# A new slot plan for windowed attention followed by a two-layer SMELU network

## The chip, the core and the metric

The kernel runs on one core of a Trainium2 chip. The metric is device time in microseconds, from the launch of the program to its end, as the median of several runs. One execution was also taken by the hardware profiler; its page and trace are read here.

The engines by their names in the profile: PE is TensorE (matmuls; PEld its weight loads), ACT is ScalarE, DVE is VectorE, POOL is GpSimd, SP is SyncE. In this kernel POOL issues all loads and SP issues the stores and the transposing transfers.

## What is computed

```python
# q, k, v: 8 batches, 8 heads, 576 positions, 64 wide
scores = matmul(q, k.T) / sqrt(64)
scores = where(|i - j| <= 32, scores, -1e9)
attn = exp(scores - max) / sum(exp(scores - max))
x = matmul(attn, v)              # regrouped to 4608 tokens x 512
h = x @ w_in                     # 512 x 2048
g = where(h >= 1, h, where(h <= -1, 0, (h + 1)**2 / 4))
out = g @ w_out                  # 2048 x 512, result 4608 x 512
```

## The kernel before

**Slots.** The kernel is one long list of 160 numbered slots, written out by hand (L505 to L566), because the order in which instructions are written is the order in which each engine runs them. Slots 0 to 143 each make one 128x512 tile of h: a projection on TensorE (L499: eight matmuls of 256 columns; in the wide slots 56 to 135 L524: four of 512) and then its SMELU. The last 16 slots have no projection left.

**SMELU, two forms.** Always ScalarE first: rr = relu(h/2 + 1/2) (L543). Then either VectorE does both of max(h, rr) and min(rr, 1) times that (L549, L550), or, in the slots named in `two_on_act`, ScalarE squares rr (L546) and VectorE does one instruction (L547). I call these Square slots. The tile of h lies in PSUM in one of two buffers, so the projection of slot a+2 waits until slot a's readers, rr and the max (or L547), are done.

**Products with w_out.** `unit` (L459) is one matmul of 512 columns of the second layer, `pair` (L474) eight matmuls of 256 columns, used early while only half of w_out is loaded. They come after the projection of a slot. Sixteen units make one 128x512 tile of the result; ScalarE copies it out of PSUM and SP stores it. Before: four units per slot in slots 24 to 39 (through `post`), three in 40 to 71, four after. The slot of each pair is listed in `pairs`.

**Attention events.** `scores` (L231, exponent on ScalarE L239, band mask, and the helper sum `both` on VectorE, L244) and `sums` (L304: numerators and denominators; then Ln and Exp of the denominator on ScalarE, L310 and L311, and a product on VectorE, L316, that writes xT) are put at positions by `at`; position a is after the projection of slot a, a + 0.5 after its products. `seq` lists, for batches 1 to 7, five sums and five scores each; `sl` gives the slots of the later ones. The product into xT is held back in `muls` and issued by `flush` at the next slot's start. `run` issues the events of a position: the matmuls of all of them, the scores with their Exp, and then, in a loop at the end, Ln and Exp of each sums.

**The mask, two forms.** With `eng` None the mask is added on TensorE by four extra matmuls (`add_mask`, L210); else VectorE multiplies the exponentials by a 0/1 mask (L205), which GpSimd prepares once (L156 to L159). Before: TensorE in slots under 14.

**Transfers.** Loads are issued by POOL in written order (L133 to L161). Eight completion semaphores take turns, so an issue waits until the one eight earlier has landed. For batch 0 q and k come in halves (`load_half`), for batch 1 in rows (`load_rows`), both transposed on TensorE (`tposes`, L191); from batch 2 on `load_nat` loads them as they lie and `xpose` (L198) transposes them by a DMA that SP issues, at the slots in `xps`. SP runs its stores and transposes in written order. q buffers of one batch and k buffers of the next take turns, so a load waits for the transpose that read the buffer before.

Of the kernel before, what the change touches and what calls it, by code (L numbers as in the profile page):

```python
# [14 lines left out]
def kernel(  # L15
# [20 lines left out]
    B, H, S, D = q.shape  # L36
    NT, DM, DFF = out.shape[0], 512, 2048
# [3 lines left out]
    MAIN = 480  # L41
    TAIL = S - MAIN
# [7 lines left out]
    nat = ctx.enter_context(tc.tile_pool(name="nat", bufs=2))  # L50
# [6 lines left out]
    ps_s = ctx.enter_context(tc.tile_pool(name="ps_s", bufs=1, space=bass.MemoryType.PSUM))  # L57
    ps_n = ctx.enter_context(tc.tile_pool(name="ps_n", bufs=1, space=bass.MemoryType.PSUM))
# [44 lines left out]
    def load_v(b, n):  # L103
        if b not in vn:
            vn[b] = nat.tile([128, 2 * NC, 2, D], BF, name="vn", tag="vn", bufs=3)
        h, a = divmod(n, 2)
        y = NY * h + 2 * a
        nc.gpsimd.dma_start(out=vn[b][64 * a:64 * a + 64, :, h], in_=v[b, y:y + 2].rearrange("y s d -> (y s) d")  # L108
                            .rearrange("(c r) d -> r c d", r=64))
# [15 lines left out]
    for h in range(2):  # L125
# [8 lines left out]
    load_v(0, 0)  # L134
    P.affine_select(out=step, in_=step, compare_op=ALU.is_ge, fill=-1.0, base=-65, channel_multiplier=-1,
                    pattern=[[1, 257]])
    for n in range(1, 4):
        load_v(0, n)
    V.memset(ones, 1.0)
    for t in qTs:  # L140
        V.memset(t[:, 0:PAD], 0.0)
# [1 line left out]
    V.tensor_sub(band, step[:, 65:], step[:, :192])  # L143
    V.tensor_scalar(bias, band, 1.0, 2.0 ** 100, op0=ALU.subtract, op1=ALU.mult)

    def put(todo):
        for fn, *x in todo:
            fn(*x)

    cuts = [0, 256, 512, 768, 1024, 1280, 1536, DFF]  # L150
    w = [(load_w_in, c0, c1, h) for c0, c1 in zip(cuts, cuts[1:]) for h in range(2)]
    w[3] += ((0, 52, 64),)
    put(w[:4] + [(load_half, 1, t, h) for t in range(2) for h in range(2)] + w[4:])
    put([(load_w_out, 0, k, k + 4) for k in (0, 4, 8)] + [(load_rows, 1, t) for t in range(2)] + [(load_w_out, 0, 12, 16)])
    put([(load_v, 1, n) for n in range(4)])
    P.tensor_copy(band[HD[1], 0:128], band[HD[1], 64:192])  # L156
    for m, n, x in ((mask4, 8, 128), (mask8, 4, TAIL)):
        P.tensor_copy(m.rearrange("p (n j) -> p n j", n=n),
                      band[:, :x].rearrange("p (n j) -> p n j", n=1).to_broadcast([128, n, x]))  # L159
    put([(load_w_out, 1, 8 * n, 8 * n + 8) for n in range(2)])  # L160
    put([(load_nat, 2, t) for t in range(2)] + [(load_v, 2, n) for n in range(4)])  # L161


    kT = {}

# [161 lines left out]
    TB = 256  # L327
# [55 lines left out]
    ps_o = ctx.enter_context(tc.tile_pool(name="ps_o", bufs=2, space=bass.MemoryType.PSUM))  # L383
# [3 lines left out]

    NB = NT // TB
    NF = DFF // 256
    pairs = [(7, 0), (7, 1), (8, 2), (11, 4), (12, 5), (13, 3), (15, 6), (15, 8), (16, 7), (17, 9)]  # L390
    two_on_act = (1, 7, 10, 11, 12)
    ev = {}

    def at(a, *todo):


        ev.setdefault(a, []).extend(x for x in todo if x)

    def steps(b, cut):

        for k, (lo, hi) in enumerate(((0, cut), (cut, MAIN))):
            for y1 in range(2):
                yield (sums, b, y1, lo, hi), (scores, b, (y1, y1 + 1), (0, 2), (2 * k, 2 * k + 2))
        yield (sums, b, 0, MAIN, S), (scores8, b)

    at(1, (tposes, 0, (0, 1), (1, 1)))
    at(2, (scores, 0, (0, 1), (0, 2), (2, 4)), (scores8, 0, ps_o))
    at(3, (scores, 0, (1, 2), (0, 2), (2, 4), ps_n), (sums, 0, 0, TB, MAIN, ps_s))
    at(4, (sums, 0, 1, TB, MAIN))
    at(5, (sums, 0, 0, MAIN, S, ps_s))  # L410
    seq = [x for b in range(1, B) for x in steps(b, CUT)]
    at(12.5, seq[0][1])
    at(13, (*seq[1][1], ps_n))
    at(14, (*seq[0][0], ps_s), seq[1][0])
    at(16, seq[2][1])
    for n, a in enumerate((18, 20, 26.5, 28)):
        at(a, seq[2 + n][0])
    for n, a in enumerate((18, 20, 26.5, 28)):
        at(a, seq[3 + n][1])
    sl = [30, 32, 35, 39, 42, 45, 47, 50, 52, 57, 60, 63, 66, 68, 72, 76, 79, 82, 86]  # L420
    sl += [90, 93, 96, 100, 104, 108, 111, 114, 118, 123]
    for n, a in enumerate(sl):
        at(a, seq[6 + n][0], seq[7 + n][1] if n < len(sl) - 1 else None)
    for t in range(2):
        at(10 + 1.5 * t, (tposes, 1, (t, 0), (t, 1)))
    two_on_act += tuple(a + 2 for a in sl)
    loads, xps = {}, {16: [(2, 0)], 18: [(2, 1)]}
    for b in range(LONG + 1, B):
        a = sl[5 * (b - 1) - 7] - 17
        for t in range(3):  # L430
            loads.setdefault(a + t, []).append((b, t))
        for t in range(2):
            xps.setdefault(a + 6 + 2 * t, []).append((b, t))

    op = {}

# [46 lines left out]
    def run(pos):  # L483
        todo = []
        for fn, *x in ev.get(pos, []):
            if fn is sums:
                todo.append(sums(*x))
            elif fn is tposes:
                tposes(*x)
            else:  # L490
                pool = (x.pop(),) if x[-1] in (ps_s, ps_n, ps_o) else ()
                fn(*x, eng, *pool)
        for end in todo:
            end()

# [5 lines left out]
                             skip_group_check=True)  # L501

    hps = []
    done = 4 * (40 - NF)
    for a in range(NF * NB + 2 * NF):  # L505
        wide = WIDE[0] <= a < WIDE[1]
        eng = None if a < 14 else V
        post = [] if a >= 40 else [x for n, x in pairs if n == a] + [a - NF] * (a >= 2 * NF + 2)
        for b, x in loads.get(a, []):
            if x < 2:  # L510
                load_nat(b, x)
            else:
                for n in range(4):
                    load_v(b, n)
        if a == 0 or a > 3:
            flush()
        if a < NF * NB:
            if wide:
                n, f = divmod(a - WIDE[0], 2 * NF)
                t = WIDE[0] // NF + 2 * n  # L520
                r0 = TB * t % RING
                hp = ps_h.tile([128, 2, TB], FP, name="hp", tag="hp")
                for n, kk in enumerate((0, 2, 1, 3)):
                    nc.tensor.matmul(hp.rearrange("p n t -> p (n t)"), w_in[:, kk, 128 * f:128 * f + 128],  # L524
                                     xT[:, kk, r0:r0 + 2 * TB], start=n == 0, stop=n == 3)
                g = gT[:, f, home(t):home(t + 1) + 1:home(t + 1) - home(t)]
            else:
                t, f = divmod(a, NF)
# [12 lines left out]

            rr = ewp.tile([128, 2, TB], FP, name="rr")
            A.activation(rr, hp, AF.Relu, scale=0.5, bias=0.5)  # L543
            mx = ewp.tile([128, 2, TB], FP, name="mx")
            if a in two_on_act:
                A.activation(mx, rr, AF.Square)  # L546
                V.scalar_tensor_tensor(g, hp, 1.0, mx, op0=ALU.max, op1=ALU.min)  # L547
            else:
                V.tensor_max(mx, hp, rr)  # L549
                V.scalar_tensor_tensor(g, rr, 1.0, mx, op0=ALU.min, op1=ALU.mult)  # L550
        flush()
        run(a)
        for x in post:
            if x < 16:
                pair(x)
            else:
                for j in range(4):
                    unit(4 * x + j)
        if a >= 40:
            n = 3 if a < 72 else 4  # L560
            for x in range(done, done + n):
                unit(x)
            done += n
        run(a + 0.5)
        for x in xps.get(a, []):
            xpose(*x)  # L566
# [30 lines left out]
```

## Time and profile before

| | |
|---|---|
| median of 3 runs | 307.9 us (307.62 to 308.05) |
| profiled execution | 307.01 us, span 305.2 us from first to last instruction |
| granted TensorE clock | 1.000 |
| SMELU max L549, product L550 | 110 each, 689 and 694 ns |
| SMELU Square L546, product L547 | 34 each, 630 and 690 ns |
| ScalarE rr L543 | 144, 594 ns |
| mask product L205 | 33; 686 ns for 128x1024, 352 ns for 128x384 |
| scores' Exp L239 | 33; 1022 ns for 128x1024 |
| bias matmuls L210 | 32 |

The page gives for each engine the busy time, then the chain of work that ended last, followed back from the last instruction, then groups of instructions by line with what ended the idle time ahead of them. A line such as `26.12 1.92 PE hp L499 x16` of the chain is start, duration, engine, tile, line and count, all in microseconds from the span's start. The end of a matmul in the trace is modelled, its start is measured. A transfer's landing is the last of its completion updates.

The start of a slot is the start of its projection's first matmul: slot 2 at 18.38, slot 6 at 26.12, slot 14 at 42.33, slot 26 at 66.08, slot 32 at 78.82, slot 40 at 95.63, slot 72 at 152.52, slot 124 at 253.19 us.

### The profile page before, as it was taken

How to read it: one execution, taken by the hardware profiler on the slowest of the kernel's cores; microseconds unless marked ns; L12 is line 12 of the kernel's file. 1: busy time of each engine (PE TensorE's matmuls, PEld its weight loads, DVE VectorE, ACT ScalarE, POOL GpSimd, SP SyncE). 2: the span in 40 equal slices, each digit the busy share in tenths (PEclk: the TensorE clock that was granted, in tenths of full speed). 3: DMA queues.
4: the chain of work that ended last, by engine and by line, in shares of the span. 5: the costliest groups of instructions: out<-in, count | busy, mean ns of one | idle time of the engine just before them, and what ended most of it. 6: DMA issues, size and time to landing. Idle time of an engine off the chain costs nothing.

```text
span 305.2 us, 7779 instructions
## 1 busy us (share of the span) xinstructions
PE 296.6 (97%) x3268; PEld 172.1 (56%) x3268; DVE 232.4 (76%) x377; ACT 208.0 (68%) x347; POOL 77.5 (25%) x93
## 2 busy tenths in 40 slices
PE   8889999999999999999999999999999999999995
PEld 3467878876566667545444444444445444446644
DVE  4269878989888898999888878877888877788700
ACT  3677786738877888788877877786778755444311
POOL 8895771019008107303700640000000000000000
PEclk9999999999999999999999999999999999999999
DMA  9999999999999999996999998570101000000121
GB/s 151 182 180 200 187 183 172 173 165 147 135 213 90 172 159 128 150 147 121 165 133 156 120 173 82 113 114 34 37 34 38 37 35 37 35 34 34 63 77 69
DMA packets 137251, 35.66 MB, mean 117 GB/s; under 512 B 122240, under 2 KB 132992, under 8 KB 137216
## 3 DMA queue, kind: packets, MB, share of 16 engines
q0 software_dynamic: 103056, 18.06, 80.5%
q1 hardware_dynamic: 34016, 16.81, 27.2%
q8 instruction: 25, 0.41, 0.6%
q10 hardware_dynamic: 144, 0.29, 0.4%
q14 instruction: 10, 0.08, 0.1%
HBM read 36.70 MB, written 9.44 MB: 151 GB/s over the span
## 4 chain that ended last, share of the span: by engine, by line
PE 84%; DMA 4%; DVE 4%; POOL 4%; ACT 2%; issue 1%; POOLq 0%; ACTq 0%
PE op L459 33%; PE hp L524 23%; PE hp L499 14%; PE op L474 5%; PE bb L304 5%; DMA w_in<-in_moe_w_in_dram 4%; POOL w_in L113 2%; PE bb L231 2%; DVE mx L549 1%; PE op L450 1%; POOL vn L108 1%; ACT pt L239 1%; DVE gT L550 1%; PE tp L191 1%; DVE xT L316 1%
## 5 line engine op out<-in xcount | busy, mean ns | idle before, releaser
L543 ACT ACTIVATE rr<-hp 128x512 f32<-128x512 f32 x144 | 85.5, 594 | 68.5 <-PE hp L524 37.7
L459 PE MATMUL op<-w_out,gT 128*128 128x512 bf16 x496 | 127.0, 380 | 0.0
L549 DVE TENSOR_TENSOR mx<-hp,rr 128x512 f32<-128x512 f32 x110 | 75.8, 689 | 26.1 <-ACT rr L543 25.3
L524 PE MATMUL hp<-xT,w_in 128*128 128x512 bf16 x320 | 82.1, 379 | 0.0
L550 DVE SCALAR_TENSOR_TENSOR gT<-rr,mx 128x512 bf16<-128x512 f32 x110 | 76.4, 694 | 3.8
L459 PEld LDWEIGHTS <-gT 128*128 128x128 bf16 x496 | 46.0, 98 | 47.6
L499 PE MATMUL hp<-xT,w_in 128*128 128x256 bf16 x512 | 66.4, 273 | 3.3 <-DMA w_in<-in_moe_w_in_dram 2.1
L499 PEld LDWEIGHTS <-w_in 128*128 128x128 bf16 x512 | 49.1, 98 | 19.0 <-issue 3.2
L524 PEld LDWEIGHTS <-w_in 128*128 128x128 bf16 x320 | 31.2, 98 | 38.2 <-issue 0.9
L100 POOL DMA_DIRECT2D qn<-in_q_dram x12 | 14.6, 1223 | 91.7 <-DMA kT<-kn 89.6
L239 ACT ACTIVATE pt<-bb 128x1024 bf16<-128x1024 f32 (+1 forms) x33 | 32.8, 999 | 3.5 <-PE bb L231 2.2
L547 DVE SCALAR_TENSOR_TENSOR gT<-hp,mx 128x512 bf16<-128x512 f32 x34 | 23.5, 690 | 13.9 <-ACT mx L546 13.6
L108 POOL DMA_DIRECT2D vn<-in_v_dram x32 | 27.5, 893 | 6.1 <-DMA w_out<-in_moe_w_out_dram 3.2
L463 ACT COPY osb<-op 128x512 f32<-128x512 f32 x31 | 18.0, 579 | 12.0 <-PE op L459 11.6
L316 DVE TENSOR_TENSOR xT<-bb,rc 128x512 bf16<-128x512 f32 (+1 forms) x32 | 20.9, 654 | 5.7 <-ACT rc L311 5.6
L311 ACT ACTIVATE rc<-lr 128x512 f32<-128x512 f32 (+2 forms) x40 | 23.5, 588 | 1.3
L310 ACT ACTIVATE lr<-bb 128x512 f32<-128x512 f32 (+2 forms) x40 | 22.0, 550 | 0.2 <-PE bb L304 0.2
L546 ACT ACTIVATE mx<-rr 128x512 f32<-128x512 f32 x34 | 21.4, 630 | 1.1
L205 DVE TENSOR_TENSOR pt<-pt,mask 128x1024 bf16<-128x1024 bf16 (+1 forms) x33 | 20.3, 615 | 1.4 <-ACT pt L239 1.4
L304 PE MATMUL bb<-pt,vn 64*64 64x128 bf16 (+3 forms) x712 | 18.7, 207 | 0.0
L304 PEld LDWEIGHTS <-vn 64*64 64x64 bf16 x712 | 14.7, 107 | 4.9 <-issue 4.7
L474 PE MATMUL op<-w_out,gT 128*128 128x256 bf16 x128 | 16.4, 273 | 0.0
(63 smaller groups left out, 167.2 us busy)
## 6 DMA issues: line engine op xcount, KB each, us to landing
out_dram<-osb SPq DMA_DIRECT2D x35, 256.0 KB, 2.8
vn<-in_v_dram POOLq DMA_DIRECT2D x32, 144.0 KB, 11.2
qn<-in_q_dram POOLq DMA_DIRECT2D x12, 288.0 KB, 6.2
kn<-in_k_dram POOLq DMA_DIRECT2D x12, 288.0 KB, 8.8
w_in<-in_moe_w_in_dram POOLq DMA_DIRECT2D x11, 128.0 KB, 5.1
w_out<-in_moe_w_out_dram POOLq DMA_DIRECT2D x4, 256.0 KB, 9.2
w_out<-in_moe_w_out_dram POOLq DMA_DIRECT2D x2, 512.0 KB, 12.3
kh<-in_k_dram POOLq DMA_DIRECT2D x4, 144.0 KB, 5.1
```

The costliest lines, as they stand in the source:

```text
L108: nc.gpsimd.dma_start(out=vn[b][64 * a:64 * a + 64, :, h], in_=v[b, y:y + 2].rearrange("y s d -> (y s) d") .rearrange("(c r) d -> r c d", ...
L239: A.activation(p, ps[:, :, :w * n].rearrange(like, y=m), AF.Exp, scale=D ** -0.5)
L304: nc.tensor.matmul(bb[HD[h], a, o + c0:o + c1], ones[HD[a]] if c is None else vn[b][HD[a], c, h], p(a, h), start=n == 0, stop=True, skip_g ...
L311: A.activation(rc[:, :, :D0], lr[:, :, :D0], AF.Exp, scale=-1.0)
L316: muls.append(lambda: V.tensor_mul(o, bb[:, :, :D0], rc[:, :, :D0]))
L459: nc.tensor.matmul(op[tt], gT[:, j, home(tt // 2), 128 * (tt % 2):128 * (tt % 2) + 128], w_out[:, j], start=j == 0, stop=j == 15)
L474: nc.tensor.matmul(o[:, tt], gT[:, j, p, 128 * tt:128 * tt + 128], w_out[:, j, 256 * half:256 * half + 256], start=not done, stop=len(done ...
L499: nc.tensor.matmul(hp[:, j], w_in[:, kk, 256 * f + 128 * j:256 * f + 128 * j + 128], xT[:, kk, r0:r0 + TB], start=first and n == 0, stop=l ...
L524: nc.tensor.matmul(hp.rearrange("p n t -> p (n t)"), w_in[:, kk, 128 * f:128 * f + 128], xT[:, kk, r0:r0 + 2 * TB], start=n == 0, stop=n == 3)
L543: A.activation(rr, hp, AF.Relu, scale=0.5, bias=0.5)
L549: V.tensor_max(mx, hp, rr)
L550: V.scalar_tensor_tensor(g, rr, 1.0, mx, op0=ALU.min, op1=ALU.mult)
```

## The change

The plan is written anew, as tables; the work itself (projections, SMELU tiles, products, scores, sums, transfers) is the same set.

- `LOADS` names every load in order. One half of the first w_in block goes ahead of the last three value tiles of batch 0; the halves of batch 0 and the w_in blocks from 768 on are interleaved differently; one value tile of batch 1 goes ahead of the last w_out block of the first half; k of batch 2 comes before q, with a value tile between.
- Masks on VectorE from position 11.5 on, instead of slot 14.
- Events: transposes of batch 0's second half at 0.5 instead of 1; the sums of slots 4 and 5 together at 5.5; the scores of 12.5 and 13 together at 12.5; those of 16 at 15.5; 18 and 20 become 18.5 and 20.5; at 28 the scores come before the sums; a new list `sl` of the same 29 entries.
- `two_on_act` is a list of its own, 27 slots instead of 34.
- `pairs` names all sixteen pairs (before, the last six followed from the slot number), and `units` gives the number of w_out products of each slot, 0 to 7, in all 512 as before.
- `ends_first`: at these positions Ln and Exp of a sums are issued right after its matmuls, ahead of the scores that follow in the same event.
- The transposes of later batches (`xps`) get slots of their own, k before q for batch 2; the loads of a batch (`loads`) too.

```diff
+    LOADS = [('w', 0, 256, 0), ('v', 0, 1), ('v', 0, 3), ('v', 0, 2), ('w', 0, 256, 1), ('w', 256, 512, 0), ('w', 256, 512, 1, (0, 52, 64)), ('half', 1, 0, 1), ('half', 1, 1, 0), ('half', 1, 0, 0), ('half', 1, 1, 1), ('w', 512, 768, 0), ('w', 512, 768, 1), ('w', 1024, 1280, 0), ('w', 768, 1024, 1), ('w', 768, 1024, 0), ('w', 1280, 1536, 0), ('w', 1280, 1536, 1), ('w', 1024, 1280, 1), ('w', 1536, 2048, 0), ('w', 1536, 2048, 1), ('o', 0, 0, 4), ('o', 0, 4, 8), ('o', 0, 8, 12), ('rows', 1, 0), ('rows', 1, 1), ('v', 1, 0), ('o', 0, 12, 16), ('v', 1, 3), ('v', 1, 2), ('v', 1, 1), ('masks',), ('o', 1, 0, 8), ('o', 1, 8, 16), ('nat', 2, 1), ('v', 2, 1), ('nat', 2, 0), ('v', 2, 2), ('v', 2, 3), ('v', 2, 0)]
...
-    for n in range(1, 4):
-        load_v(0, n)
...
-    put(w[:4] + [(load_half, 1, t, h) for t in range(2) for h in range(2)] + w[4:])
-    put([(load_w_out, 0, k, k + 4) for k in (0, 4, 8)] + [(load_rows, 1, t) for t in range(2)] + [(load_w_out, 0, 12, 16)])
-    put([(load_v, 1, n) for n in range(4)])
...
-    put([(load_nat, 2, t) for t in range(2)] + [(load_v, 2, n) for n in range(4)])
...
+    for kind, *x in LOADS:
+        kinds[kind](*x)
...
-    pairs = [(7, 0), (7, 1), (8, 2), (11, 4), (12, 5), (13, 3), (15, 6), (15, 8), (16, 7), (17, 9)]
-    two_on_act = (1, 7, 10, 11, 12)
+    pairs = [(6, 0), (7, 1), (8, 2), (11, 4), (12, 5), (13, 3), (14, 6), (15, 8), (17, 7), (17, 10), (18, 9), (19, 13), (19, 15), (21, 14), (22, 11), (23, 12)]
...
-    sl = [30, 32, 35, 39, 42, 45, 47, 50, 52, 57, 60, 63, 66, 68, 72, 76, 79, 82, 86]
-    sl += [90, 93, 96, 100, 104, 108, 111, 114, 118, 123]
...
-    two_on_act += tuple(a + 2 for a in sl)
-    loads, xps = {}, {16: [(2, 0)], 18: [(2, 1)]}
+    for a, *names in [(0.5, 't0'), (2, 'c0', 'c2'), (3, 'c1', 's0'), (5.5, 's1', 's2'), (10, 'tq'), (11.5, 'tk'), (12.5, (1, 0), 'C1'), (14, 'S0', (0, 1)), (15.5, (1, 2)), (18.5, (0, 2), (1, 3)), (20.5, (0, 3), (1, 4)), (26.5, (0, 4), (1, 5)), (28, (1, 6), (0, 5))]:
...
+    two_on_act = [6, 10, 11, 13, 16, 22, 25, 28, 30, 34, 41, 44, 47, 51, 59, 62, 64, 74, 90, 96, 109, 122, 123, 126, 127, 131, 132]
+    sl = [30, 35, 37, 39, 42, 45, 47, 49, 52, 58, 60, 63, 65, 68, 71, 77, 79, 81, 85, 89, 92, 95, 101, 103, 108, 110, 112, 115, 117]
+    first_sl = 6
+    bias_until = 11.5
+    ends_first = [0.5, 2.5, 3, 4, 10, 11.5, 12.5, 14, 15.5, 20, 36, 49, 75, 89, 93, 116, 118, 123]
...
+    for t, a in enumerate([16, 15]):
+        xps.setdefault(a, []).append((2, t))
...
-            xps.setdefault(a + 6 + 2 * t, []).append((b, t))
+            xps.setdefault([[28, 30], [40, 44], [58, 59], [75, 79], [91, 98]][b - 3][t], []).append((b, t))
...
             if fn is sums:
                 todo.append(sums(*x))
+                if pos in ends_first:
+                    todo.pop()()
...
-                fn(*x, eng, *pool)
+                fn(*x, None if pos < bias_until else V, *pool)
...
+    units = [0, 0, 0, 0, 0, 0, 0, 0, 0, 0, 0, 0, 0, 0, 0, 0, 0, 0, 0, 0, 0, 0, 0, 0, 5, 3, 5, 4, 5, 3, 6, 5, 0, 4, 4, 5, 4, 4, 3, 3, 3, 4, 3, 3, 3, 3, 2, 4, 3, 1, 5, 3, 2, 3, 4, 3, 2, 3, 4, 2, 4, 3, 3, 3, 4, 3, 3, 2, 4, 3, 4, 1, 4, 6, 2, 5, 2, 4, 5, 3, 4, 4, 5, 4, 6, 2, 2, 7, 2, 4, 6, 4, 4, 2, 4, 3, 5, 4, 5, 4, 6, 1, 3, 6, 4, 5, 4, 3, 3, 5, 5, 2, 4, 7, 2, 4, 0, 4, 5, 6, 3, 6, 3, 7, 4, 2, 5, 4, 3, 4, 4, 4, 4, 4, 5, 4, 2, 4, 6, 3, 4, 3, 4, 4, 5, 2, 4, 4, 6, 5, 4, 5, 3, 2, 3, 3, 4, 7, 4, 4]
...
-        eng = None if a < 14 else V
-        post = [] if a >= 40 else [x for n, x in pairs if n == a] + [a - NF] * (a >= 2 * NF + 2)
...
-        if a >= 40:
-            n = 3 if a < 72 else 4
-            for x in range(done, done + n):
-                unit(x)
-            done += n
+        for x in range(done, done + units[a]):
+            unit(x)
+        done += units[a]
```

More of the change, by code (lines that the diff above doesn't have):

```diff
@@ L144, with masks @@
     V.tensor_scalar(bias, band, 1.0, 2.0 ** 100, op0=ALU.subtract, op1=ALU.mult)
[L146 to L152, printed above, removed]
-    put(w[:4] + [(load_half, 1, t, h) for t in range(2) for h in range(2)] + w[4:])
-    put([(load_w_out, 0, k, k + 4) for k in (0, 4, 8)] + [(load_rows, 1, t) for t in range(2)] + [(load_w_out, 0, 12, 16)])
-    put([(load_v, 1, n) for n in range(4)])
[L156 to L160, printed above, removed]
-    put([(load_nat, 2, t) for t in range(2)] + [(load_v, 2, n) for n in range(4)])
+    def masks():
+        P.tensor_copy(band[HD[1], 0:128], band[HD[1], 64:192])
+        for m, n, x in ((mask4, 8, 128), (mask8, 4, TAIL)):
+            P.tensor_copy(m.rearrange("p (n j) -> p n j", n=n),
+                          band[:, :x].rearrange("p (n j) -> p n j", n=1).to_broadcast([128, n, x]))
+    kinds = {"v": load_v, "w": load_w_in, "half": load_half, "o": load_w_out, "rows": load_rows, "nat": load_nat, "masks": masks}
+    for kind, *x in LOADS:
+        kinds[kind](*x)
     kT = {}
@@ L404, in steps @@
         yield (sums, b, 0, MAIN, S), (scores8, b)
[L406 to L410, printed above, removed]
-    seq = [x for b in range(1, B) for x in steps(b, CUT)]
[L412 to L419, printed above, removed]
-    sl = [30, 32, 35, 39, 42, 45, 47, 50, 52, 57, 60, 63, 66, 68, 72, 76, 79, 82, 86]
-    sl += [90, 93, 96, 100, 104, 108, 111, 114, 118, 123]
-    for n, a in enumerate(sl):
-        at(a, seq[6 + n][0], seq[7 + n][1] if n < len(sl) - 1 else None)
-    for t in range(2):
-        at(10 + 1.5 * t, (tposes, 1, (t, 0), (t, 1)))
-    two_on_act += tuple(a + 2 for a in sl)
@@ L427 @@
-    loads, xps = {}, {16: [(2, 0)], 18: [(2, 1)]}
+    seq = [x for b in range(1, B) for x in steps(b, CUT)]
+    early_items = {"t0": (tposes, 0, (0, 1), (1, 1)), "c0": (scores, 0, (0, 1), (0, 2), (2, 4)), "c2": (scores8, 0, ps_o),
+                   "c1": (scores, 0, (1, 2), (0, 2), (2, 4), ps_n), "s0": (sums, 0, 0, TB, MAIN, ps_s),
+                   "s1": (sums, 0, 1, TB, MAIN), "s2": (sums, 0, 0, MAIN, S, ps_s),
+                   "tq": (tposes, 1, (0, 0), (0, 1)), "tk": (tposes, 1, (1, 0), (1, 1)),
+                   "C1": (*seq[1][1], ps_n), "S0": (*seq[0][0], ps_s)}
@@ new lines @@
+    for a, *names in [(0.5, 't0'), (2, 'c0', 'c2'), (3, 'c1', 's0'), (5.5, 's1', 's2'), (10, 'tq'), (11.5, 'tk'), (12.5, (1, 0), 'C1'), (14, 'S0', (0, 1)), (15.5, (1, 2)), (18.5, (0, 2), (1, 3)), (20.5, (0, 3), (1, 4)), (26.5, (0, 4), (1, 5)), (28, (1, 6), (0, 5))]:
+        for x in names:
+            at(a, early_items[x] if isinstance(x, str) else seq[x[1]][x[0]])
+    two_on_act = [6, 10, 11, 13, 16, 22, 25, 28, 30, 34, 41, 44, 47, 51, 59, 62, 64, 74, 90, 96, 109, 122, 123, 126, 127, 131, 132]
@@ new lines @@
+    sl = [30, 35, 37, 39, 42, 45, 47, 49, 52, 58, 60, 63, 65, 68, 71, 77, 79, 81, 85, 89, 92, 95, 101, 103, 108, 110, 112, 115, 117]
+    first_sl = 6
+    bias_until = 11.5
+    ends_first = [0.5, 2.5, 3, 4, 10, 11.5, 12.5, 14, 15.5, 20, 36, 49, 75, 89, 93, 116, 118, 123]
+    for n, a in enumerate(sl):
+        at(a, seq[first_sl + n][0], seq[first_sl + 1 + n][1] if first_sl + 1 + n < len(seq) else None)
+    loads, xps = {}, {}
+    for t, a in enumerate([16, 15]):
+        xps.setdefault(a, []).append((2, t))
@@ L428 @@
     for b in range(LONG + 1, B):
-        a = sl[5 * (b - 1) - 7] - 17
+        a = [20, 31, 49, 72, 88][b - 3]
         for t in range(3):
@@ L503 @@
     hps = []
-    done = 4 * (40 - NF)
+    done = 64
+    units = [0, 0, 0, 0, 0, 0, 0, 0, 0, 0, 0, 0, 0, 0, 0, 0, 0, 0, 0, 0, 0, 0, 0, 0, 5, 3, 5, 4, 5, 3, 6, 5, 0, 4, 4, 5, 4, 4, 3, 3, 3, 4, 3, 3, 3, 3, 2, 4, 3, 1, 5, 3, 2, 3, 4, 3, 2, 3, 4, 2, 4, 3, 3, 3, 4, 3, 3, 2, 4, 3, 4, 1, 4, 6, 2, 5, 2, 4, 5, 3, 4, 4, 5, 4, 6, 2, 2, 7, 2, 4, 6, 4, 4, 2, 4, 3, 5, 4, 5, 4, 6, 1, 3, 6, 4, 5, 4, 3, 3, 5, 5, 2, 4, 7, 2, 4, 0, 4, 5, 6, 3, 6, 3, 7, 4, 2, 5, 4, 3, 4, 4, 4, 4, 4, 5, 4, 2, 4, 6, 3, 4, 3, 4, 4, 5, 2, 4, 4, 6, 5, 4, 5, 3, 2, 3, 3, 4, 7, 4, 4]
     for a in range(NF * NB + 2 * NF):
         wide = WIDE[0] <= a < WIDE[1]
-        eng = None if a < 14 else V
-        post = [] if a >= 40 else [x for n, x in pairs if n == a] + [a - NF] * (a >= 2 * NF + 2)
         for b, x in loads.get(a, []):
@@ L552 @@
         run(a)
-        for x in post:
-            if x < 16:
+        for n, x in pairs:
+            if n == a:
                 pair(x)
-            else:
-                for j in range(4):
-                    unit(4 * x + j)
-        if a >= 40:
-            n = 3 if a < 72 else 4
-            for x in range(done, done + n):
-                unit(x)
-            done += n
+        for x in range(done, done + units[a]):
+            unit(x)
+        done += units[a]
         run(a + 0.5)
```

## The prediction

> **What bounds the kernel now.** I read the engines' busy times first, then the chain that ended last, then busy time by stretch, and last the starts of the matmuls one after another.
>
> ```profile
> PE 296.6 (97%) x3268; PEld 172.1 (56%) x3268; DVE 232.4 (76%) x377; ACT 208.0 (68%) x347; POOL 77.5 (25%) x93
> ...
> PE 84%; DMA 4%; DVE 4%; POOL 4%; ACT 2%; issue 1%; POOLq 0%; ACTq 0%
> ```
>
> TensorE is busy 97% and is 84% of the chain. But a 512-column matmul shows as 380 ns while four of them follow each other in 0.86 us (216 ns each), so "busy" hides gaps of up to 0.16 us behind each; gaps must be read from starts.
>
> ```profile
> 18.62 7.45 DMA w_in<-in_moe_w_in_dram
> 26.07 0.05 issue
> 26.12 1.92 PE hp L499 x16
> ...
> 79.09 0.63 DVE xT L316
> 79.72 0.04 issue
> 79.76 0.81 PE hp L499 x6
> ```
>
> Two different regimes stand here. Up to 26.07 us the last w_in transfer sets when slot 6 may start, whatever TensorE does before. After it, only single waits remain: at 79.76 slot 32 waits for xT.
>
> ```profile
> 26.20:95.60 69.40, 68.84 (x952) 52.26 (x953) 58.35 (x95) 50.00 (x84) 25.67 (x27) 1.00 1.67 166
> 95.60:152.50 56.90, 56.63 (x681) 32.80 (x680) 50.90 (x83) 47.95 (x82) 21.60 (x22) 1.00 1.77 149
> 152.50:255.00 102.50, 102.50 (x998) 48.36 (x997) 83.04 (x133) 75.33 (x126) 8.26 (x8) 1.00 0.70 83
> ```
>
> Columns: stretch, length, then busy time of PE, PEld, DVE, ACT, POOL, the granted clock, DMA share, GB/s. The rows are slots 6 to 39, 40 to 71 and 72 to 123. VectorE is nearest to being a bound in the middle one: 50.90 of 56.90, 6.0 idle; that is also where a slot has only three w_out products.
>
> ```profile
> 110.98 0.81 PE L459 MATMUL op<-w_out,gT 128*128 128x512 bf16 x3
> 111.63 1.04 PE L499 MATMUL hp<-xT,w_in 128*128 128x256 bf16 x8
> 112.50 0.81 PE L459 MATMUL op<-w_out,gT 128*128 128x512 bf16 x3
> 113.55 1.03 PE L499 MATMUL hp<-xT,w_in 128*128 128x256 bf16 x8 [0.24 <-DVE mx L549]
> ```
>
> Three products, then the next slot: 0.65 us from start to start at 110.98, 1.05 at 112.50. So slot 50 came 0.40 late, because the max of slot 48 had not yet freed its PSUM buffer. Read like this, all waits of TensorE after 26.1 us are: 0.72 (slot 32), 0.40 (50), 0.19 (71), 0.17 (55), and six of 0.07 to 0.09; 1.9 us in all. That, plus TensorE work that is left out, is nearly all that a reordering can win there.
>
> **The change, part by part** (against the profiled execution, 307.01 us with span 305.2; the median of the runs, 307.9, is 0.9 above it).
>
> *Masks from slot 12.* The scores of slots 12.5 and 13 lose four bias matmuls each. The trace has them start at 39.33 and 40.88 and the scores behind them at 39.57 and 41.12: 2 x 0.24 = **-0.48 us** of TensorE. VectorE gets two mask products instead (0.686 each by L205, 1.37 in all), hidden by its idle time there (39.86, 41.08 and 41.61 start after waits of 0.68, 0.53 and 0.18); uncovered they would cost 1.37. The masks are copied on GpSimd at 31.05 to 32.53, long before. Their place in the load list, after the values of batch 1, stays.
>
> *Both scores in one event at 12.5.* An excursion to attention costs a gap going in and one coming out: the eight projections from 39.90 (0.87) could end at 40.77, the bias starts at 40.88 (0.11); 16 score matmuls at about 14 ns from 41.12 end at 41.34, the next product starts at 41.44 (0.10). One excursion less: **-0.20**.
>
> *Load order.* One w_in half goes ahead of the last three value transfers, so the last value tile lands one transfer later: landings 10.78 and 11.40, so +0.62. The sums that wait for it start later, xT is ready at 13.97 instead of 13.35, and the first four projections (0.44) end near 14.5. The second w_in block lands at 14.64 in either order, and slot 0 waits for it: cost 0, uncovered 0.62. The same transfers stand ahead of the last w_in half, so 26.07 stays; unknown to plus or minus one landing, 0.65. The batch-1 rows keep their place (landing 32.93 and 35.83, used at 33.29 and 36.27).
>
> *Sums at 5.5, transposes at 0.5, Squares before slot 6*: all before 26.07, hidden by the w_in wait (0.81 us of TensorE idle just before). Without that cover the copies moved ahead of slot 1's SMELU would cost that slot up to 1.33 us (L194's two copies on ScalarE).
>
> *Batch 2's k rows before its q rows, and its transposes k first.* SyncE issues a transpose in 6.48 and 6.70 us, in order, and the second lands at 66.69; the scores of slot 26.5 start at 68.22. Slack 1.5; TensorE comes 0.7 earlier: 0, priced below as a rival. A w_out store (slot 17 instead of 16) now stands behind both transposes on SyncE and leaves some 13 us later; three output buffers carry that.
>
> *w_out products.* 512 remain 512, 0.216 us each: 0 by themselves. By slot 31 four more are done (the running count stands at 100 against 96), and slot 32 has none: 0.86 us of work stands ahead of the wait of 0.72. With TensorE 0.68 earlier from the first two items, and with slots 28 and 30 made Square slots (2 x 0.69 less on VectorE, which is busy 10.48 of the 11.21 us before that wait), I take **-0.65**. In slots 40 to 71 counts go from a flat 3 to 1 to 5, so single slots have 0.2 to 0.4 more cover just before a late PSUM buffer and less elsewhere. Of the 1.1 us there I take half, **-0.50**. Bounds for both: 0 and -1.9; and below nothing, the next item.
>
> *SMELU slots.* The words of the change say more ScalarE, but the Square slots fall from 34 to 27: 8 to 10 up to slot 39, 11 to 7 in slots 40 to 71, 15 to 10 after. Each slot that leaves the list costs VectorE 689 + 694 - 690 = 0.693 us and frees 0.630 of ScalarE. After slot 72 that is 5 x 0.69 = 3.5 against 19.5 idle: 0. In slots 40 to 71 it is 4 x 0.693 = 2.8 on 50.9, with 56.9 - 1.0 = 55.9 to fit in. It fits, and a wait goes with it:
>
> ```profile
> DVE gT L547 <- ACT mx L546: 1.1, 4, 0.4
> ```
>
> I take 0; with all 6.0 idle kept it costs 2.8 (rival below).
>
> [...] The rows above have VectorE at 81 to 89% of the stretches, TensorE at 99 to 100%, so I follow the rows.
>
> *Ln/Exp first.* Of the listed positions only 49 and 89 hold sums followed by scores; elsewhere nothing moves. There the mask product waits for 592 + 630 ns more of ScalarE, xT is no later. Bounds -0.3 to +1.2, taken 0, since both engines idle in those slots.
>
> *Sum*: -0.48 - 0.20 - 0.65 - 0.50 = -1.83. The profiled execution goes from 307.0 to 305.2, the median from 307.9 to **306.1 us**.
>
> **Rivals.**
>
> *VectorE becomes the bound in slots 40 to 71.* Its idle time there is mostly waits for ScalarE, and those may all stay while 2.8 us of work is added: the stretch takes 50.9 + 2.8 + 6.0 = 59.7 instead of 56.9. Then the 0.50 isn't won: 307.9 + 2.8 - 1.3 = 309.4. For: 89% busy, every listed wait there ends at a max (L549). Against: Square waits leave with the Squares. It decides once more than 3.2 us of VectorE idle are kept there.
>
> *A transfer gives it back.* Batch 2's q now follows a value tile, 1.2 to 2.4 us later by neighbouring landings (56.16, 57.37, 59.76), so scores at slot 26.5, due at 67.5, wait until 67.9 to 69.1: 0.4 to 1.6, say 1.0: 307.1. For: DMA is 90% busy in all slices to 70 us. Against: both transposes landed only after the value tiles did (64.83), whichever is first.
>
> *The waits only move.* TensorE loses its 0.68 us of work, and what is filled in one slot is missing in the next: 307.9 - 0.7 = 307.2. For: the number of products is the same. Against: slots without an event have about 1 us to spare after slot 72.
>
> **How the numbers follow.** Forecast 0.50 (own range 305.3, everything recovered, to 307.0), VectorE bound 0.22, transfer 0.16, waits move 0.12. A change under 0.2%, 0.6 us, can't be told from none: the limit is 307.3. Faster: 0.50 + 0.06 + 0.08 = 0.64; same: half of the two middle rivals, 0.14; slower 0.22. Range: below 305.3 only if a w_in landing comes earlier (to 304.9); above, into the VectorE case, to 308.8.
>
> **What would show it.** Right: slot 6 still starts near 26.1; no bias matmuls after slot 11; slot 32 starts without a wait on xT; L549 holds PE up less than 0.6 us in all; 27 Squares. Wrong: a PE wait on transposed q or k near 67 us; slots 40 to 71 longer than 56.9 with VectorE over 95%; or a w_in landing off 26.07 by more than 0.65.

## The result, and the profile after

| | before | changed |
|---|---|---|
| median of 12 runs each, same chip | 307.81 us (306.02 to 308.98) | 305.60 us (304.78 to 306.97) |
| ratio, 95% interval | | 0.9942 [0.992, 0.9963] |
| profiled execution, span | 307.01, 305.2 us | 306.23, 304.5 us |
| SMELU max and product / Square slots | 110 / 34 | 117 / 27 |

By the ratio the change makes the kernel faster by 0.58%, 1.8 us (1.1 to 2.5); the medians lie 2.2 apart, since the times of both scatter over 2 to 3 us. Beside that the two profiled executions are only 0.8 us apart: the one before lies 0.8 below its median, the one after 0.6 above. So the stretches are read one by one. First two lines of the changed kernel's page, busy times and the shares of the chain that ended last:

```profile
PE 294.8 (97%) x3260; PEld 172.2 (57%) x3260; DVE 236.5 (78%) x386; ACT 202.3 (66%) x340; POOL 77.9 (26%) x93
...
PE 83%; DMA 9%; POOL 4%; ACT 1%; DVE 1%; issue 1%; POOLq 0%; ACTq 0%; DVEq 0%
```

VectorE has 4.1 us more and ScalarE 5.7 us less, mainly the seven Square slots that changed hands. VectorE's share of the chain fell from 4% to 1%; DMA's rose from 4% to 9%. The chain itself (start, duration, what) says which transfers:

```profile
20.71 10.44 DMA w_out<-in_moe_w_out_dram
...
31.19 1.03 PE op L461 x8
...
79.05 1.08 PE op L446 x5
80.13 1.75 PE hp L488 x16
...
106.42 11.80 DMA kT<-kn
```

At 80.13 slots 32 and 33 follow each other and nothing is waited for: the wait on xT is gone. In its place stand two transfers that the chain before didn't have: w_out for the early pairs (31.19) and a transposed k (106.42). Busy time by stretch, columns as before, at nearly the same cuts:

```profile
26.20:96.00 69.80, 69.17 (x952) 52.85 (x950) 58.80 (x95) 52.52 (x89) 26.40 (x27) 1.00 1.79 168
96.00:152.60 56.60, 56.26 (x715) 32.82 (x713) 52.35 (x87) 45.09 (x77) 21.22 (x22) 1.00 1.72 146
152.60:255.00 102.40, 102.40 (x962) 48.17 (x960) 87.43 (x141) 68.97 (x117) 8.26 (x8) 1.00 0.71 86
```

In the middle row VectorE has 52.35 of 56.60, where it had 50.90 of 56.90: 92% busy. Slots 40 to 71 alone take 57.50 instead of 56.89 us, but they hold one event (its scores and sums) and one product more; up to slot 73, with the same events, the stretch is not longer (table below). Its own waits there (the waits of VectorE, us in all, times, longest) show why there was room:

```profile
DVE gT L535 <- ACT mx L534: 1.7, 6, 0.4
DVE mx L537 <- ACT rr L531: 0.9, 4, 0.4
```

The second line was 2.8 us in 11 waits before. TensorE's waits from 26.2 us on are these four, and none is for a max:

```profile
PE op L461 <- DMA w_out<-in_moe_w_out_dram: 0.6, 2, 0.3
PE hp L488 <- DMA w_in<-in_moe_w_in_dram: 0.2, 1, 0.2
PE bb L222 <- DMA kT<-kn: 0.2, 1, 0.2
PE bb L295 <- DVE xT L307: 0.2, 1, 0.2
```

Now where each stretch's time went, from the starts of slots in the traces of all kernels (the profiled execution of each; us):

| kernel | span | slot 6 starts | 6 to 10 | 10 to 24 | 24 to 40 | 40 to 73 | 73 to 124 | 10 to end |
|---|---|---|---|---|---|---|---|---|
| before | 305.2 | 26.12 | 6.20 | 30.28 | 33.03 | 59.37 | 98.19 | 272.93 |
| changed | 304.5 | 25.93 | 7.01 | 30.02 | 32.02 | 59.23 | 98.63 | 271.52 |
| changed, again (e5) | 303.7 | 25.39 | 6.63 | 30.13 | 32.02 | 59.25 | 98.63 | 271.65 |
| e1 flat products | 308.3 | 29.68 | 6.13 | 30.03 | 32.80 | 58.98 | 98.59 | 272.45 |
| e2 34 Squares | 308.0 | 26.80 | 8.29 | 30.36 | 32.66 | 59.46 | 98.85 | 272.94 |
| e3 bias to 14 | 306.7 | 29.05 | 6.62 | 29.96 | 32.02 | 58.84 | 98.63 | 271.06 |
| e4 pairs later | 302.6 | 25.28 | 6.20 | 30.02 | 32.02 | 58.84 | 98.63 | 271.13 |
| e6 old load order | 303.2 | 25.51 | 6.51 | 30.04 | 32.02 | 58.84 | 98.63 | 271.16 |
| e7 products alone | 305.4 | 25.22 | 6.26 | 30.28 | 32.78 | 59.77 | 99.50 | 273.94 |
| e8 Squares alone | 305.2 | 25.82 | 6.12 | 30.41 | 32.87 | 59.70 | 98.19 | 273.22 |
| e9 old loads, later pairs | 302.6 | 25.27 | 6.12 | 30.05 | 32.02 | 58.85 | 98.63 | 271.16 |
| e10 events alone | 305.7 | 26.00 | 6.42 | 30.36 | 33.02 | 59.62 | 98.19 | 273.24 |
| e11 half bias | 302.3 | 25.33 | 6.13 | 29.75 | 32.02 | 58.84 | 98.63 | 270.85 |
| e12 ends after | 303.3 | 25.60 | 6.56 | 30.03 | 32.02 | 58.84 | 98.63 | 271.15 |

The traces of e5, e6 and e9 to e12 lack four or five records of projection matmuls; their weight loads are complete and mark the slots there. In e1, e2 and e3 a stretch of half clock (granted 0.51, 0.50 and 0.50) lies between slots 4 and 10 (last section), so their columns ahead of slot 10, and their spans, are not compared with the others. Stretches that don't hold the same number of products aren't comparable as they stand. The new table has one product less in slots 24 to 39, one more in 40 to 72, two more in 73 to 123, at 0.216 us each. Cleared of that, the change wins 0.26, then 1.01 - 0.22 = 0.79, then 0.14 + 0.22 = 0.36, then nothing (0.44 more for 0.43 of products); 1.4 us from slot 10 to the end. Ahead of slot 10 it loses 0.8 in slots 6 to 9 (0.4 in the second execution, e5). Those 0.8 are on TensorE's timeline (start, duration, engine, operation, idle before):

```profile
25.93 1.05 PE L488 MATMUL hp<-xT,w_in 128*128 128x256 bf16 x8 [0.24 <-DMA w_in<-in_moe_w_in_dram]
27.32 1.03 PE L461 MATMUL op<-w_out,gT 128*128 128x256 bf16 x8 [0.34 <-DMA w_out<-in_moe_w_out_dram]
28.19 1.04 PE L488 MATMUL hp<-xT,w_in 128*128 128x256 bf16 x8
...
31.19 1.03 PE L461 MATMUL op<-w_out,gT 128*128 128x256 bf16 x8 [0.22 <-DMA w_out<-in_moe_w_out_dram]
```

Eight matmuls take 0.87. The pair at 27.32 could have started at 26.80 and the one at 31.19 at 30.80: 0.52 and 0.39 late for w_out blocks that land at 27.27 and 31.15.

### The profile page after: what moved, and what is told of

The parts are those of the page before. It is cut to its first block, busy times and chain, and to the rows that moved or that the text cites. A ratio compares the mean times of both kernels' runs of the same rounds, so it can differ in the third digit from the quotient of the medians.

```text
span 304.5 us, 7762 instructions
## 1 busy us (share of the span) xinstructions
PE 294.8 (97%) x3260; PEld 172.2 (57%) x3260; DVE 236.5 (78%) x386; ACT 202.3 (66%) x340; POOL 77.9 (26%) x93
## 4 chain that ended last, share of the span: by engine, by line
PE 83%; DMA 9%; POOL 4%; ACT 1%; DVE 1%; issue 1%; POOLq 0%; ACTq 0%; DVEq 0%
PE op L446 35%; PE hp L512 23%; PE hp L488 13%; PE bb L295 4%; DMA kT<-kn 4%; PE op L461 4%; DMA w_out<-in_moe_w_out_dram 3%; POOL w_in L114 2%; PE bb L222 2%; DMA w_in<-in_moe_w_in_dram 2%; PE op L437 1%; POOL vn L109 1%; PE tp L182 1%; ACT pt L230 1%; POOL w_out L119 0%
## 5 line engine op out<-in xcount | busy, mean ns | idle before, releaser
L537 DVE TENSOR_TENSOR mx<-hp,rr 128x512 f32<-128x512 f32 x117 | 80.5, 688 | 20.9 <-ACT rr L531 19.5
L538 DVE SCALAR_TENSOR_TENSOR gT<-rr,mx 128x512 bf16<-128x512 f32 x117 | 81.2, 694 | 4.0
L535 DVE SCALAR_TENSOR_TENSOR gT<-hp,mx 128x512 bf16<-128x512 f32 x27 | 18.6, 691 | 11.7 <-ACT mx L534 11.0
L196 DVE TENSOR_TENSOR pt<-pt,mask 128x1024 bf16<-128x1024 bf16 (+1 forms) x35 | 21.7, 620 | 3.1 <-ACT pt L230 3.0
L534 ACT ACTIVATE mx<-rr 128x512 f32<-128x512 f32 x27 | 17.0, 630 | 0.9
```

## The experiments

All were timed beside the kernel before on the same chip. Edits are to the changed kernel unless said otherwise. A ratio of the changed kernel itself stands in two places: 0.9942 above and 0.9947 below.

### What the counts and the Squares are worth inside the plan

**e1**: old counts of products.

```diff
+    units = [0] * 24 + [4] * 16 + [3] * 32 + [4] * 88
```

> The changed kernel, only with the old flat counts of w_out products (4 in slots 24 to 39, 3 in 40 to 71, 4 after). Theory (the uneven counts fill waits): slot 32 waits for xT again (up to 0.7 us) and slots 40 to 71 have the same 1 us of waits or more, so 1.0 to 1.8 us slower than the changed kernel, 306.6 to 307.4 for the median, ratio to before 0.996 to 0.999. Rival (the counts only move waits, the gain is in the masks, the merged event and the start): within 0.4 us of the changed kernel, ratio 0.993 to 0.996.

Measured: 307.06 us, 0.9992 [0.997, 1.0013]: the gain is gone. TensorE's timeline at slot 32:

```profile
81.98 0.38 PE L488 MATMUL hp<-xT,w_in 128*128 128x256 bf16 x2
82.77 0.81 PE L488 MATMUL hp<-xT,w_in 128*128 128x256 bf16 x6 [0.41 <-DVE xT L307]
```

Two matmuls take 0.22 from start to start, here 0.79: the wait of slot 32 is back with 0.57. From slot 10 to the end, with the same work in both, the kernel is 0.93 us longer than the changed one; 0.78 of it lies in slots 24 to 39, where it also has one product (0.22) more. The changed kernel also has a wait at slot 52 that e1 has not (below, under slots 40 to 71); without it the loss would be 1.3. So the four products done earlier ahead of slot 32 are what removed that wait, as forecast.

**e2**: the old rule for Square slots, 34 of them.

```diff
-    two_on_act = [6, 10, 11, 13, 16, 22, 25, 28, 30, 34, 41, 44, 47, 51, 59, 62, 64, 74, 90, 96, 109, 122, 123, 126, 127, 131, 132]
+    two_on_act = [1, 7, 10, 11, 12] + [a + 2 for a in sl]
```

> The changed kernel, only with the old rule for Square slots (34: 1, 7, 10, 11, 12 and two after each event of the new list). Theory (VectorE had room, seven Squares less cost nothing): VectorE busy falls by 4.9 us and the time stays within 0.4 us, ratio 0.993 to 0.996. Rival 1 (VectorE is close to the bound in slots 40 to 71): 0.5 to 2 us faster, ratio under 0.992. Rival 2 (a Square slot frees its PSUM buffer later, so fewer of them is itself a gain): 0.4 to 1 us slower, ratio 0.996 to 0.998.

Measured: 307.55 us, 1.0004 [0.9983, 1.0025]. VectorE gets 7 x 0.69 us less to do, 50.25 instead of 52.35 in the stretch from 96.0 to 152.6, and the kernel is 0.6% slower than the changed one. From slot 10 on it loses 1.42 us (1.8 against e4, which doesn't have the changed kernel's wait at slot 52), and the two largest of TensorE's waits there (36 us on) are for products of VectorE:

```profile
PE op L461 <- DVE gT L538: 0.6, 1, 0.6
PE hp L488 <- DVE gT L535: 0.3, 1, 0.3
```

L535 is the product of a Square slot. It comes after two passes on ScalarE (0.594 and 0.630) where another slot's max needs one, and it is what frees the PSUM buffer. That explains the second line; that the rest has the same cause is argued, not shown. So although VectorE is 92% busy in that stretch of the changed kernel, the seven slots that e2 moves to ScalarE cost time.

**e5**: the changed kernel once more, to have it beside the next three.

> The changed kernel itself, unchanged, beside the others of this job on one chip. If its gain is that of the plan and not of the executions drawn: ratio 0.992 to 0.996. The profile shows what varies between executions: the last w_in landing anywhere from 25.2 to 28.2 us (as in the profiles so far), and slot 6 with it.

Measured: 305.58 us, 0.9947 [0.9926, 0.9968].

**e7** and **e8** put one of the two alone into the kernel before: e7 the new counts, e8 the new Square list.

```diff
+        for x in range(done, done + units[a]):
+            unit(x)
+        done += units[a]
```

```diff
-    two_on_act += tuple(a + 2 for a in sl)
+    two_on_act = [6, 10, 11, 13, 16, 22, 25, 28, 30, 34, 41, 44, 47, 51, 59, 62, 64, 74, 90, 96, 109, 122, 123, 126, 127, 131, 132]
```

> The kernel before, only with the new counts of w_out products per slot. Theory (the counts are fitted to the new events and Squares and help only with them): 0 to 1 us slower than before, or equal, ratio 0.999 to 1.004. Rival (they fill the waits by themselves, that of slot 32 first): 0.7 to 1.5 us faster, ratio 0.995 to 0.998.

> The kernel before, only with the new list of 27 Square slots. Theory (a Square slot frees its PSUM buffer 0.6 us later; fewer of them in slots 40 to 71 is itself a gain): 0.3 to 1 us faster, ratio 0.996 to 0.999. Rival (the list fits only the new events): equal or slower, ratio 1.000 to 1.005. If VectorE were the bound in slots 40 to 71: 1 us slower or more, ratio over 1.003.

Measured: e7 308.21 us, 1.0037 [1.0012, 1.0062]; e8 308.61, 1.0042 [1.0015, 1.0068]. Each alone makes the kernel slower. In e7 the wait of slot 32 is gone too (0.66 us), so the counts alone remove it; but it comes back as a wait of slot 35. TensorE's timeline of e7 there:

```profile
82.31 1.04 PE L499 MATMUL hp<-xT,w_in 128*128 128x256 bf16 x8
83.18 1.03 PE L459 MATMUL op<-w_out,gT 128*128 128x512 bf16 x4
84.67 1.03 PE L499 MATMUL hp<-xT,w_in 128*128 128x256 bf16 x8 [0.46 <-DVE mx L550]
```

Four products take 0.86 from start to start; slot 35 follows 1.49 after 83.18, 0.63 late. This is the rival that the waits only move, at work where the counts stand without the new events and Squares. TensorE's waits of e7 (60 us on), then its timeline at slots 116 and 117:

```profile
PE hp L499 <- DVE mx L550: 0.7, 2, 0.5
PE hp L525 <- DVE mx L550: 0.6, 1, 0.6
```

```profile
237.65 1.03 PE L525 MATMUL hp<-xT,w_in 128*128 128x512 bf16 x4
239.25 1.02 PE L525 MATMUL hp<-xT,w_in 128*128 128x512 bf16 x4 [0.58 <-DVE mx L550]
```

Slot 116 has no product in the new table. Four wide matmuls end their turn 0.86 after 237.65, at 238.51; slot 117 starts at 239.25, 0.74 late, for a max; in the changed kernel slot 117 follows slot 116 after 0.86 with the same count. So it is the old events and Squares that make this max late; which of them isn't shown. TensorE's and VectorE's timelines of e8 show the mirror image:

```profile
140.62 0.81 PE L459 MATMUL op<-w_out,gT 128*128 128x512 bf16 x3
141.80 1.02 PE L524 MATMUL hp<-xT,w_in 128*128 128x512 bf16 x4 [0.37 <-DVE gT L547]
```

```profile
140.02 0.68 DVE L316 TENSOR_TENSOR xT<-bb,rc 128x512 bf16<-128x512 f32 x1
141.06 0.69 DVE L547 SCALAR_TENSOR_TENSOR gT<-hp,mx 128x512 bf16<-128x512 f32 x1 [0.35 <-ACT mx L546]
```

A Square slot's product ends at 141.75 and the projection behind it starts at 141.80, where it could have at 141.27 (140.62 and three products of 0.216): 0.53 late; 0.09 of it the kernel before had at this slot. Most times of e7 and e8 fall into two groups 2 us apart (for e8 306.9 to 307.6 and 309.0 to 309.4, with one between); the traces are of the lower groups, and what makes the upper ones isn't known. In these traces e7 loses 1.01 and e8 0.29 us after slot 10.

**e10**: the rest alone, that is the changed kernel with both old lists (the edits of e1 and e2).

> The changed kernel with the old flat product counts and the old rule of 34 Square slots together: what stays new is the loads, the events, the masks, the pairs and Ln/Exp first. Theory (counts, Squares and events fit only together): from slot 10 to the end 272.5 to 273.5 us (the changed kernel 271.6, the one before 272.9), ratio 0.998 to 1.003. Rival (each of the two reversions alone broke a fit; both together restore the old fit): as the changed kernel, ratio 0.994 to 0.996.

Measured: 307.57 us, 0.9994 [0.9964, 1.0023]: by the runs the same as the kernel before; in the trace it is 0.31 longer after slot 10. So the three parts give +0.31 (events and loads), +1.01 (counts) and +0.29 (Squares) in the traces, +1.6 us if they added up. Together they give -1.4.

### What the early part is worth

**e3**: bias matmuls instead of mask products up to slot 14.

```diff
-    bias_until = 11.5
+    bias_until = 14
```

> The changed kernel, only with the band mask of the two scores at 12.5 added by eight bias matmuls on TensorE as before. Theory of the prediction: 0.48 us slower (TensorE work), slot 14 starts 0.48 later. Rival: in the trace of the changed kernel the sums of slot 14 start 0.4 us late behind the mask products on VectorE; with the bias that wait goes, and from slot 15 on nothing is lost: within 0.1 us.

Measured: 305.56 us, 0.9968 [0.9943, 0.9992], which the runs can't tell from the changed kernel; 10 to 24 takes 29.96 instead of 30.02. The scores of 12.5 cost 0.43 more (1.00 from their first matmul to the next projection, 0.57 in the changed kernel), and the sums behind them cost less. What the changed kernel pays at the sums stands on two engines, TensorE and VectorE:

```profile
43.24 0.21 PE L295 MATMUL bb<-pt,ones 64*64 64x32 bf16 x4
...
43.67 0.21 PE L295 MATMUL bb<-pt,ones 64*64 64x32 bf16 x4
43.70 0.30 PE L295 MATMUL bb<-pt,vn 64*64 64x96 bf16 x8
44.06 0.28 PE L295 MATMUL bb<-both,ones 64*64 64x192 bf16 x4
```

```profile
41.93 0.69 DVE L196 TENSOR_TENSOR pt<-pt,mask 128x1024 bf16<-128x1024 bf16 x1 [0.71 <-ACT pt L230]
42.65 0.36 DVE L235 TENSOR_TENSOR both<-pt 128x384 bf16<-128x384 bf16 x1
42.93 0.69 DVE L196 TENSOR_TENSOR pt<-pt,mask 128x1024 bf16<-128x1024 bf16 x1
43.65 0.36 DVE L235 TENSOR_TENSOR both<-pt 128x384 bf16<-128x384 bf16 x1
```

Two mask products and two folds (L235) follow each other without a gap from 41.93 to 44.01. The sums start at 43.24, catch up with them, and the group that needs the second fold starts at 44.06, right behind it. From the first sums matmul to the last group's start (44.14) it is 0.90 here and 0.53 in e3 (46.41 to 46.94).

**e4**: the first pairs later, when their w_out blocks are there.

```diff
-    pairs = [(6, 0), (7, 1), (8, 2), (11, 4), (12, 5), (13, 3), (14, 6), (15, 8), (17, 7), (17, 10), (18, 9), (19, 13), (19, 15), (21, 14), (22, 11), (23, 12)]
+    pairs = [(7, 0), (7, 1), (9, 2), (11, 4), (12, 5), (13, 3), (14, 6), (15, 8), (17, 7), (17, 10), (18, 9), (19, 13), (19, 15), (21, 14), (22, 11), (23, 12)]
```

> The changed kernel, only with pair 0 back in slot 7 and pair 2 in slot 9 instead of 8. In the trace of the changed kernel these two wait for the first and third w_out transfer, 0.50 and 0.39 us beyond their start. Theory (TensorE is the bound from 26.1 us on, so these waits are lost for good): slot 9 or 10 starts some 0.5 to 0.8 us earlier and the kernel is 0.5 to 0.8 us faster, median near 305.0, ratio 0.992. Rival (the wait at slot 14 for the mask products or the transposes of batch 2 take it up): same time, within 0.2 us.

Measured: 304.38 us, 0.992 [0.9892, 0.9948], from 6 runs. Slots 6 to 9 take 6.20 instead of 7.01, and at slot 40 the difference is still there. In the traces the two kernels then differ in slot 52 alone; by the runs the gain over the changed kernel (0.9942) is not clear of noise, since the intervals overlap.

**e6**: the old load order.

```diff
+    LOADS = [('v', 0, 1), ('v', 0, 2), ('v', 0, 3), ('w', 0, 256, 0), ('w', 0, 256, 1),
...
+        ('rows', 1, 0), ('rows', 1, 1), ('o', 0, 12, 16), ('v', 1, 0), ('v', 1, 1), ('v', 1, 2), ('v', 1, 3),
...
```

> The changed kernel, only with all loads in the order of the kernel before. Theory of the prediction (load order costs and brings nothing, the same transfers stand ahead of the last w_in): within 0.4 us of the changed kernel, slot 6 at the last w_in landing. Rival (the w_in block of slot 4 comes two transfers later in the new order; in two of the profiles slot 4 started at 25.4 us behind it): slot 4 starts near 22 us again, and the kernel is 0.3 to 1.5 us faster than the changed one. Rival 2 (the new order is a gain, values or k of batch 2 were late): 0.4 us slower or more.

Measured: 304.90 us, 0.9951 [0.9924, 0.9978], the same as e5 within the intervals: no part of the gain is seen to come from the order of the loads.

**e9**: e6 and e4 together.

> The changed kernel with all loads in the old order, and pair 0 in slot 7, pair 2 in slot 9. Theory (the steady part from slot 10 on is the plan's gain, the start only loses by the early pairs): slot 10 near 31.5 us, from slot 10 to the end 271.1 to 271.6 us, and the time 0.4 to 1.0 us under the changed kernel, ratio to before 0.990 to 0.993. Rival (the start is the transfers' and nothing in it is lost): as the changed kernel, ratio 0.994 to 0.996.

Measured: 304.44 us, 0.9898 [0.9864, 0.9932], from 8 runs. Its timeline of TensorE has no gap after slot 6's wait:

```profile
25.27 1.92 PE L488 MATMUL hp<-xT,w_in 128*128 128x256 bf16 x16 [0.27 <-DMA w_in<-in_moe_w_in_dram]
27.02 1.91 PE L461 MATMUL op<-w_out,gT 128*128 128x256 bf16 x16
28.77 1.91 PE L488 MATMUL hp<-xT,w_in 128*128 128x256 bf16 x16
```

**e11**: e9, and of the two scores at 12.5 one with bias matmuls, one with the mask product, so that neither engine has both.

```diff
-                fn(*x, None if pos < bias_until else V, *pool)
+                fn(*x, None if pos < bias_until or (pos == 12.5 and pool) else V, *pool)
```

> As e9_order_and_pairs, and of the two scores at 12.5 the second has its mask added by four bias matmuls again, the first keeps the product on VectorE. Theory (slot 14 waits for the last mask product): the bias costs 0.24 us, the wait of 0.27 at slot 14 goes, so equal to e9 within 0.2 us. Rival (the wait belongs to the first scores): 0.2 to 0.3 us slower than e9.

Measured: 304.19 us (303.79 to 307.29), 0.9901 [0.9867, 0.9934]. After slot 10 it is 0.31 shorter than e9, 0.30 of it in 10 to 24, which neither expectation had; TensorE's timeline shows the bias on the one score and the sums no longer interrupted (eight groups from 41.98 to 42.51):

```profile
38.71 0.39 PE L201 MATMUL bb<-bias,ident 64*64 64x512 bf16 x4
...
41.98 0.21 PE L295 MATMUL bb<-pt,ones 64*64 64x32 bf16 x4
...
42.51 0.26 PE L295 MATMUL bb<-pt,vn 64*64 64x128 bf16 x8
```

By the runs, e9 and e11 can't be told apart; both beat the kernel before by 1.0%. Their ratios lie 0.4% under that of the changed kernel, but the intervals overlap.

**e12**: Ln and Exp of the sums in their old place.

```diff
-    ends_first = [0.5, 2.5, 3, 4, 10, 11.5, 12.5, 14, 15.5, 20, 36, 49, 75, 89, 93, 116, 118, 123]
+    ends_first = []
```

> The changed kernel with Ln and Exp of the sums after the scores' Exp everywhere, as before. Theory of the prediction (it matters at slots 49 and 89 alone and is worth nothing): within 0.3 us of the changed kernel, and the stretch from slot 40 to 73 as there, 58.8 to 59.7 us. Rival (it frees xT earlier): slots 50 and 90 wait, 0.3 to 1.2 us slower.

Measured: 305.67 us, 0.9938 [0.9911, 0.9966]: the same as the changed kernel.

## Why the prediction was right, and where it was not

*What bounds the kernel, the sign and the size*: right. TensorE has next to no idle time after 26 us in either kernel (waits of 1.9 us in all before, 1.2 in the list above after), and the forecast of 306.1 lies 0.5 above the median of 305.6. But the closeness is in part luck, from errors that cancel: one term too good by 0.4, a loss of 0.4 to 0.8 left out, and about 1 us that the traces after slot 6 don't show and that was not forecast.

*Slot 32, -0.65*: 0.79 in the trace for slots 24 to 39, with the cause named (e1 brings 0.57 of the wait back). The counts alone move it on to slot 35 (e7); that it stays away takes the rest of the plan.

*Slots 40 to 71, -0.50*: 0.36. A new wait is in it. At slot 52 the scores need batch 4's transposed k, issued at 106.42 and landing 11.80 later (TensorE's timeline):

```profile
117.88 0.20 PE L295 MATMUL bb<-pt,vn 64*64 64x64 bf16 x4
118.27 0.42 PE L222 MATMUL bb<-qT,kT 64*64 64x128 bf16 x16 [0.19 <-DMA kT<-kn]
```

These starts were 0.03 apart before (118.50 and 118.53) and are 0.39 now. e3, e4, e6, e9, e11 and e12 don't have this wait, and their stretch is 0.39 shorter, 58.84 or 58.85: without it the term is -0.75. Both executions of the changed kernel have it, and in both the transfer took 11.8 us to land; in the six others 8.8 to 11.1. The rival of a late transpose had the right kind of wait, at batch 2 where nothing was late. What sets the time of this transfer, and so why the wait comes and goes between kernels with the same plan at slot 52, isn't settled.

*Masks and merged scores, -0.48 and -0.20*: as predicted up to slot 14, which starts 0.06 before its old time where slot 10 starts 0.62 after it: 0.68. The step that failed is the next sentence, that the two mask products are "hidden by its idle time there". VectorE had idle time, but not between the Exp and the sums that need the products; 0.4 comes back at slot 14, and 0.26 is left by slot 24. e3 parts the two: with the merged scores and the old bias, slots 10 to 13 take 9.77 instead of 10.01, so the merging is worth 0.24, and the masks, 30.02 against 29.96 up to slot 24, nothing. What counted was the length of VectorE's queue ahead of the next consumer, 4 instructions in a row, not its idle share; e11, with one mask product less in that queue, gains 0.30.

*Pairs, not costed*: the largest miss, +0.8, and +0.3 to +0.4 in the traces of e5, e6 and e12, where only the first of the two blocks came late. The prediction took the early w_out products for work that only moves, and counted waits for w_in, values and rows, not for w_out. e4 shows in its trace that two pairs one slot later win it back.

*Load order and Ln/Exp first, 0*: right as far as the runs can tell (e6, e12). Slot 0 starts at 13.87; 13.97 was expected.

*Squares, 0*: the VectorE rival is refuted: slots 40 to 71 did grow past 56.9, to 57.50, but with an event and a product more and VectorE at 92%, not over 95%; up to slot 73 the stretch is no longer. But zero is wrong too: within this plan the 27 slots are worth 1.4 us in the traces and 0.6% in the runs (e2), and outside it they cost 0.4% (e8). The prediction added terms one by one. For a table of counts, a list of Square slots and a list of events that is no sound step: which max or product is late is set by all three. The count of 0 at slot 116 is free in the changed kernel, where the buffer is already released, and costs 0.74 in e7, where it isn't.

*Open*: after slot 6 the traces give -0.6 (changed) and -0.85 (e5; spans to two places 305.25 before, 304.45 and 303.67); the runs give -1.8 and -1.6. That the remaining 1 us lies ahead of slot 6 is argued, not shown; one profiled execution of each kernel can't settle it: the last w_in block landed between 25.0 and 28.2 us over these kernels, 25.34 and 25.88 in two executions of the same one. The least times of each are 304.5 against 305.76 on one chip, 1.3 us apart.

## What to carry to other kernels

In a kernel whose TensorE is 97% busy, read waits from the starts of matmuls and compare stretch by stretch, with the work in each made equal, from a point behind the noisy start. When work is moved to an engine with idle time, look at the queue between its producer and the next consumer, not at the idle share: here 2.08 us without a gap (41.93 to 44.01) on an engine that is 78% busy. Tables that were fitted together should be tested together: here two of three parts alone cost time, the third gained nothing, and the whole won.

## What the hardware showed that was not expected

*A slower clock after one wait.* In the profiled execution of e1, and of e2 and e3, TensorE waited long for w_in near 25 us. Windows of e1 (columns as above):

```profile
22.00:25.40 3.40, 0.67 (x48) 0.55 (x37) 2.11 (x4) 2.35 (x4) 1.21 (x2) 0.99 1.16 169
25.40:28.80 3.40, 3.39 (x16) 2.18 (x16) 0.82 (x2) 0.60 (x1) 2.49 (x3) 0.51 1.43 198
28.80:32.20 3.40, 3.40 (x80) 3.05 (x80) 2.84 (x5) 3.13 (x6) 1.88 (x3) 1.00 1.25 206
```

After 3.4 us in which it was busy 0.67 and waited 2.74 in one piece, TensorE worked 3.4 us at half clock (0.51): 16 matmuls where the next window, at 1.00, has 80, of all sizes. An estimate from these 3.4 us is that it costs up to 1.7 us of the 2.3 to 3.0 by which those three profiled executions lie above their medians. In e3 TensorE was busy 0.30 of the 2.80 us up to 25.3, and the granted clock was 0.91, 0.50 and 0.62 in the next three windows, up to 30.5; in e2 a wait of 1.65 us, up to 26.80, was followed by a clock of 0.50 from 28.2 to 31.6. In the kernel before, the changed one, e5 and e9 the longest wait for w_in from 20 us on was 0.62, 0.24, 0.38 and 0.27 us, and the clock of the whole profiled execution was 1.000; it was 0.994 in e1, e2 and e3, 0.998 in e4 and e8, 1.000 in the rest. That the wait brings on the slower clock is argued from these executions, not shown: no run varies the wait alone.

*A start that varies.* The changed kernel and e1 to e5 load in the same order. In one profiled execution of each, the last w_in block landed between 25.24 (e4) and 28.23 us (e3); in two executions of the same kernel at 25.88 and 25.34. A difference of 1 us in the start of two single profiles says nothing.
